# Dynamic convolution, Fourier mixing and MLP on one core: 64-bit weights turned into float32 by four VectorE operations and two ScalarE operations instead of seven VectorE operations

## The chip, the cores and the metric

The kernel runs on one core of a Trainium2 chip. The metric is the device time of one launch in microseconds (us), the median of several runs. TensorE multiplies matrices into PSUM; VectorE (DVE), ScalarE (ACT) and GpSimd (POOL) work elementwise; SyncE (SP) issues the DMAs.

## The reference, cut to what matters

```python
# x (8, 4224, 192) f32, weight_gen (8, 4224, 8, 7) f32, w_ch1 (192, 768) f64, w_ch2 (768, 192) f64
w = softmax(weight_gen, axis=-1)
out = np.einsum('bshk,bskhg->bshg', w, x_unf)        # 7 taps, 8 heads of 24 channels
X = np.fft.fft(np.fft.fft(x, axis=1), axis=2)        # x is that output
u = x + np.real(X).astype(np.float32)
un = (u - mean(u)) / np.sqrt(var(u) + 1e-06)
ch = np.maximum(un @ w_ch1, 0.0) @ w_ch2
return (u + ch).astype(np.float32)
```

The two weight matrices come as 64-bit floats: a float32 array times a 64-bit scalar. The kernel reads them as pairs of 32-bit words and makes float32 of them on the chip.

## The kernel before, in words

For each of 8 batches the kernel does a convolution (softmax of the taps, products on VectorE, sums on GpSimd, for batch 0 also products on ScalarE and sums on TensorE), folds rows and takes a first transform on TensorE (`spectrum`), writes the spectrum to DRAM and reads it back turned (`transform`, tiles g2, results pp), copies pp to pq on ScalarE (L945 to L956), and then for 9 groups of 512 rows mixes (`mix`, PSUM tile eo), normalises (`norm`) and runs the two matmuls of the MLP (`mlp`: L1105 into ph, relu on ScalarE into tiles hh, L1149 into po). There are 72 groups. The MLP needs the weights as pairs of float16 (w1h, w1l, w2h, w2l), and w2 first as float32 (w2f) for the first six groups.

The weights are loaded once, in six raw pieces of 128 x 384 numbers of two words each (`load_piece`), three of w1 and three of w2. `words_to_f32` (L485) turns a piece into float32 by seven VectorE operations: L492 and L494 make sign, exponent and upper mantissa from the high word, L495 and L496 set numbers too small for float32 to zero, L498 takes the power of two of the result, L501 scales the low word by it, L503 adds. `split_f32` (L506) then makes the float16 pair of a w1 piece, one ScalarE operation (L508) and one VectorE operation (L509). `prep_w1` does the three w1 pieces after the last convolution product of batch 0, `prep_w2` one w2 piece each, in the stretch before the first MLP group.

The program is written in one order, and `plan` (L175) then sets the order of every engine's queue: a list scheduler with the costs of `cost`, which ranks the operations over several walks, keeps the best walk, and links each queue in that order. `held` (L391) makes instructions wait in this order behind a given one, but only those on the same engine as that one (L204). Tiles of one tag are given out in the order in which the program first uses them: tag hh has 10 buffers (temporaries of the conversion, then the relu results), ph has 3 PSUM banks, po has 2. `keep_warm` puts 40 small matmuls (L563) on TensorE while the spectrum of batch 0 goes to DRAM and back, and 8 more after each of two mix steps.

Of the kernel before, what the change touches and what calls it, by code (L numbers as in the profile page):

```python
# [11 lines left out]
F16 = mybir.dt.float16  # L12
F32 = mybir.dt.float32
I32 = mybir.dt.int32
U32 = mybir.dt.uint32
AF = mybir.ActivationFunctionType
ALU = mybir.AluOpType
# [4 lines left out]
P = 128  # L22
# [21 lines left out]
DVE_ADDS = {(1, c): 1 for c in range(2, NC)}  # L44
HOLD3 = 3
WIRE = 0.7

F32_GROUPS = 6
WIDE_FROM = 2
# [89 lines left out]
def together(ap):  # L139

    run = 1
    for step, n in reversed(ap.ap[1:]):
        if n > 1 and step != run:
            break
        run *= n
    return run


def cost(ins, lane, reads, writes):
# [10 lines left out]
    if lane == "sp":  # L160
        if ins.opcode == "DmaTransposeAnt":
            return TURN * n / (12 * P), 2000 + 1.2 * n, 1.09 * n
        size, run = BYTES[out.dtype], min(together(ap) for ap in reads + writes)
        return 400, 2000 + WIRE * count(out) * size, out.ap[0][1] * count(out) / run * (0.5 + 0.0023 * run * size)
    if lane == "dve":
# [196 lines left out]
def tile_dynconv_fnet_mlp(  # L362
# [12 lines left out]
    nc = tc.nc  # L375
# [22 lines left out]
    def pst(tag, bufs, shape, dt, name):  # L398
        return ps.tile(shape, dt, tag=tag, name=name, bufs=bufs)
# [44 lines left out]
    PW = 2 * D  # L444
# [7 lines left out]
    def temp(nm, dt):  # L452
        return sb.tile([P, PW], dt, tag="hh", name=nm, bufs=10)
# [31 lines left out]
    def words_to_f32(raw, out, nm, bank):  # L485

        hi, lo = raw[:, :, 1], raw[:, :, 0]
        v = nc.vector
        a = pst(*bank, [P, PW], I32, f"pa_{nm}")
        w = pst(*bank, [P, PW], F32, f"pw_{nm}")  # L490
        t = temp(f"t_{nm}", I32)
        v.tensor_scalar(out=a, in0=hi, scalar1=3, scalar2=0x3FFFFFFF,  # L492
                        op0=ALU.logical_shift_left, op1=ALU.bitwise_and)
        v.scalar_tensor_tensor(out=t, in0=hi, scalar=-0x40000000, in1=a, op0=ALU.bitwise_and, op1=ALU.bitwise_or)  # L494
        v.tensor_scalar(out=a, in0=hi, scalar1=0x7FF00000, scalar2=None, op0=ALU.bitwise_and)  # L495
        v.scalar_tensor_tensor(out=w, in0=a, scalar=float(0x38100000), in1=t.bitcast(F32),  # L496
                               op0=ALU.is_ge, op1=ALU.mult)
        v.tensor_scalar(out=a, in0=w.bitcast(I32), scalar1=23, scalar2=23,  # L498
                        op0=ALU.logical_shift_right, op1=ALU.logical_shift_left)
        r = t.bitcast(F32)  # L500
        ins = v.scalar_tensor_tensor(out=r, in0=lo.bitcast(U32), scalar=2.0 ** -52, in1=a.bitcast(F32), op0=ALU.mult, op1=ALU.mult)  # L501
        out = w if out is None else out
        last_word.append(v.tensor_tensor(out=out, in0=w, in1=r, op=ALU.add))  # L503
        return out

    def split_f32(w, hi16, lo16, sc):  # L506

# [18 lines left out]
    def prep_w1(raws):  # L526
        s1 = weight_scale([raw[:, :, 1] for raw in raws], 64, "w1")
        scales.append(s1)
        hi, lo = temp("w1h_1", F16), temp("w1l_1", F16)
        w = words_to_f32(raws[0], None, "w1_1", ("ph", 3))  # L530
        split_f32(w, hi, lo, s1)
        with held(g2_loads[0, (NK1 + 2) // 3 // TRI * TRI].ins):
            for src, dst in ((hi, w1h1), (lo, w1l1)):
                for i in range(2):
                    for j in range(2):
                        nc.sync.dma_start(dst[64 * j:64 * j + 64, i * PW:(i + 1) * PW], src[64 * i:64 * i + 64])
        for i in range(2):
            cs_ = slice(i * PW, (i + 1) * PW)
            w = words_to_f32(raws[1 + i], None, f"w1_0{i}", ("ph", 3))
            split_f32(w, w1h0[:, cs_], w1l0[:, cs_], s1)  # L540

    def prep_w2(i):
        words_to_f32(loaded[1][i], w2_part(i)[0], f"w2_{i}", ("ph", 3) if i < 2 else ("po", 2))
# [653 lines left out]
    last_word, last_split, last_lo, last_bn, last_ph, scales = [], [], {}, {}, {}, []  # L1197
# [119 lines left out]
```

## Time and profile before

| what | value |
|---|---|
| time, median of 3 runs (lowest to highest) | 1079.35 us (1078.82 to 1079.69) |
| profiled execution: span from first to last instruction | 1076.2 us |
| median of the runs less that span | 3.15 us |
| TensorE busy | 1057.1 us (98%) |
| VectorE busy | 933.7 us (87%) |
| ScalarE busy | 862.9 us (80%) |
| GpSimd busy | 851.4 us (79%) |
| granted TensorE clock, mean | 0.998 |

The span is the time between the program's first and last instruction in the one execution that was profiled; the runs' times hold what lies around it too. The profile's page gives busy time by engine, the span in 40 slices, the chain of work that ended last and the costliest groups of instructions; the trace behind it can be asked for stretches, lines and tiles.

### The profile page before, as it was taken

The page shows a single profiled execution, that of the slowest core. Times are in us where ns is not written, and L with a number is a line of the kernel's source. Part 1 is how long each engine was busy: PE and PEld are TensorE (multiplying, and loading weights), DVE is VectorE, ACT ScalarE, POOL GpSimd, SP SyncE. Part 2 cuts the span into 40 slices and gives each one's busy share as a digit, 9 for nine tenths or more (in the row PEclk, how much of TensorE's full clock was granted, in tenths as well). Part 3 has the DMA queues.
Part 4 walks back from the last instruction along what each step waited for, and adds up shares of the span by engine and source line. Part 5 has one row for each costly group of instructions (what it writes and reads, how often), then busy time and mean ns, then how long its engine had stood idle before and what let it go on. Part 6 is the DMA issues. An engine that isn't in the chain of part 4 may idle for free.

```text
span 1076.2 us, 23645 instructions
## 1 busy us (share of the span) xinstructions
PE 1057.1 (98%) x8603; PEld 803.8 (75%) x8603; DVE 933.7 (87%) x1597; ACT 862.9 (80%) x2597; POOL 851.4 (79%) x616
## 2 busy tenths in 40 slices
PE   8899999999999999999999999999999999999998
PEld 5476687886778777887778777787778777886667
DVE  8999999999989998899989998899989997374433
ACT  4666875669987998889897898889897998699953
POOL 5979899899969999699959999699969999011210
PEclk9999999999999999999999999999999999999999
DMA  9453056624683458625582447734583424523221
GB/s 322 136 147 117 8 136 180 175 48 101 157 233 80 98 133 210 158 75 121 145 215 80 111 127 205 157 76 125 137 180 89 88 68 99 143 56 87 72 71 49
DMA packets 186324, 134.88 MB, mean 125 GB/s; under 512 B 134299, under 2 KB 167008, under 8 KB 186208
## 3 DMA queue, kind: packets, MB, share of 16 engines
q1 hardware_dynamic: 186208, 133.37, 48.3%
q8 instruction: 68, 1.11, 0.4%
q14 instruction: 48, 0.39, 0.1%
HBM read 61.46 MB, written 39.37 MB: 94 GB/s over the span
## 4 chain that ended last, share of the span: by engine, by line
PE 66%; POOL 15%; DVE 10%; issue 5%; ACT 2%; DMA 1%; SPq 0%; POOLq 0%; DVEq 0%; ACTq 0%
PE po L1149 28%; PE ph L1105 24%; POOL u L893 7%; POOL u L822 4%; PE pp L941 4%; PE eo L972 3%; PE ph L1072 3%; PE pg L845 3%; DVE pr L810 2%; POOL sm L836 2%; POOL hl L1048 1%; DVE pr L889 1%; DVE u L889 1%; DMA x_sb<-in_x_dram 1%; POOL hl L1050 1%
## 5 line engine op out<-in xcount | busy, mean ns | idle before, releaser
L893 POOL TENSOR_TENSOR u<-u,pr 128x1536 f32<-128x1536 f32 x144 | 497.1, 3454 | 15.4 <-DVE pr L889 13.4
L1149 PE MATMUL po<-w2h,hh 128*128 128x192 f16 x2880 | 411.2, 246 | 1.3 <-ACT po L1146 0.8
L1149 PEld LDWEIGHTS <-hh 128*128 128x128 f16 x4320 | 364.1, 98 | 61.6 <-issue 18.9
L1105 PE MATMUL ph<-ht,w1h 128*128 128x512 f16 (+1 forms) x1296 | 387.5, 362 | 2.6 <-DVE hh L1125 1.2
L1149 PE MATMUL po<-w2l,hh 128*128 128x192 f16 x1440 | 354.1, 246 | 0.0
L1125 DVE SCALAR_TENSOR_TENSOR hh<-ph,hh 128x512 f16<-128x512 f32 (+1 forms) x396 | 241.3, 634 | 77.5 <-ACT hh L1124 76.9
L889 DVE TENSOR_TENSOR pr<-x_sb,wp 128x1536 f32<-128x1536 f32 x144 | 250.2, 1743 | 6.8 <-POOL u L893 6.7
L1124 ACT ACTIVATE hh<-ph 128x512 f16<-128x512 f32 (+1 forms) x396 | 208.8, 551 | 48.5 <-PE ph L1105 27.1
L1105 PEld LDWEIGHTS <-w1h 128*128 128x128 f16 x1296 | 126.9, 100 | 94.8 <-issue 16.9
L1105 PE MATMUL ph<-ht,w1l 128*128 128x512 f16 (+1 forms) x528 | 180.4, 350 | 0.0
L1038 ACT ACTIVATE un<-u,rs 128x192 f32<-128x192 f32 x252 | 122.0, 539 | 16.4 <-POOL rs L1036 13.1
L1048 POOL TENSOR_TENSOR hl<-un,hl 128x512 f16<-128x512 f32 (+1 forms) x69 | 74.3, 1077 | 74.8 <-ACT hl L1042 39.5
L822 POOL TENSOR_TENSOR u<-u,pr 128x768 f32<-128x768 f32 (+1 forms) x72 | 115.6, 1612 | 8.8 <-DVE rs L1012 4.7
L1009 ACT ACTIVATE junk<-u,st 128x192 f16<-128x192 f32 x252 | 114.2, 453 | 3.0
L1007 ACT ACTIVATE junk<-u 128x192 f16<-128x192 f32 x252 | 90.8, 360 | 21.9 <-DVE u L981 17.5
L972 PEld LDWEIGHTS eo<-cs_sb,pq 97*128 97x128 f32 x544 | 93.4, 191 | 9.0 <-issue 1.1
L972 PE MATMUL eo<-cs_sb,pq 97*128 97x97 f32 x544 | 92.3, 265 | 0.1
L810 DVE TENSOR_TENSOR pr<-x_sb,wp 128x768 f32<-128x768 f32 (+1 forms) x91 | 74.6, 867 | 1.4 <-PE pa L815 0.7
L1105 PEld LDWEIGHTS <-w1l 128*128 128x128 f16 x528 | 52.9, 100 | 23.7 <-issue 3.7
L1036 POOL TENSOR_TENSOR rs<-st,rs 128x4 f32<-128x4 f32 (+1 forms) x69 | 14.0, 202 | 67.8 <-DVE rs L1012 63.1
L836 POOL TENSOR_TENSOR sm<-u 128x382 f32<-128x382 f32 x64 | 64.0, 1000 | 3.4 <-ACT u L689 3.2
L845 PE MATMUL pg<-sm,f_sb 128*128 128x192 f32 x256 | 55.1, 333 | 1.4 <-POOL sm L837 1.3
(143 smaller groups left out, 1585.5 us busy)
## 6 DMA issues: line engine op xcount, KB each, us to landing
out_dram<-u SPq DMA_DIRECT2D x64, 384.0 KB
x_sb<-in_x_dram SPq DMA_DIRECT2D x48, 384.0 KB
g<-g_d SPq DMA_DIRECT2D x40, 336.0 KB
x_sb<-in_x_dram SPq DMA_DIRECT2D x8, 864.0 KB
g_d<-gt SPq DMA_DIRECT2D x32, 195.0 KB
g_d<-gt SPq DMA_DIRECT2D x32, 189.0 KB
w<-in_weight_gen_dram SPq DMA_DIRECT2D x6, 924.0 KB
x_sb<-in_x_dram SPq DMA_DIRECT2D x8, 672.0 KB
```

The lines of the kernel that those rows point to most:

```text
L810: last_product[b] = nc.vector.tensor_tensor(out=dst, in0=rows, in1=wk, op=ALU.mult)
L822: adder.tensor_tensor(out=u, in0=u, in1=pr, op=ALU.add)
L889: last_product[b] = nc.vector.tensor_tensor(out=pr.rearrange("p (s r) (h g) -> p s (r h) g", s=2, g=G), in0=rows, in1=wp[:, :, :, k:k + 1] ...
L893: nc.gpsimd.tensor_tensor(out=u, in0=u, in1=pr, op=ALU.add)
L972: last_mix[b] = nc.tensor.matmul(eo[:, e, j, :], lhsT=pq[0:DH, e, r, r:r + P], rhs=cs_sb[:, e, :], start=True, stop=True)
L1007: nc.scalar.activation(junk, uv[t], AF.Identity, scale=-1.0 / D, accum_out=st[:, t, 0:1])
L1009: nc.scalar.activation(junk, uv[t], AF.Square, bias=st[:, t, 0:1], accum_out=st[:, t, 1:2])
L1038: nc.scalar.activation(un[:, t, :], uv[t], AF.Identity, bias=rs[:, 1, t:t + 1], scale=rs[:, 0, t:t + 1])
L1105: last_ph[n] = nc.tensor.matmul(ph[:, 0:T], lhsT=wt[:, cs_], rhs=ht[:, 0:T, blk], start=(i == 0 and not opens), stop=(i == len(terms) - 1 ...
L1124: nc.scalar.activation(a[:, 0:T], ph[:, 0:T], AF.Relu)
L1125: nc.vector.scalar_tensor_tensor(out=l[:, 0:T], in0=ph[:, 0:T], scalar=0.0, in1=a[:, 0:T], op0=ALU.max, op1=ALU.subtract)
L1149: nc.tensor.matmul(po[t // 2][:, t % 2, :], lhsT=hx[:, t], rhs=wx[:, c2, :], start=(c2 == 0 and i == 0 and not seeds[t // 2] and not (late ...
```

## The change

A piece is now made so: ScalarE takes the absolute value of the high word read as float32, scaled by a constant that rounds to zero in float16 below the least number kept (near), and the sign of that (keep, 0 or 1, float16). VectorE shifts the high word (as L492 does), then joins the low word's upper three bits, then sign and top exponent bit, and last multiplies by keep. The intermediate stays in one PSUM tile; the PSUM tile of the result is made only where the result isn't written to w2f directly, and the temporary t of tag hh goes, for near and keep of the same tag. The low word's other bits are dropped where the old form rounded them in.

```diff
+LEAST = float(np.float32(2.0 ** -25) / np.nextafter(np.uint32(0x38100000).view(np.float32), np.float32(0)))
 
         hi, lo = raw[:, :, 1], raw[:, :, 0]
         v = nc.vector
+        near, keep = temp(f"near_{nm}", F16), temp(f"keep_{nm}", F16)
+        nc.scalar.activation(near, hi.bitcast(F32), AF.Abs, scale=LEAST)
+        nc.scalar.activation(keep, near, AF.Sign)
         a = pst(*bank, [P, PW], I32, f"pa_{nm}")
-        w = pst(*bank, [P, PW], F32, f"pw_{nm}")
-        t = temp(f"t_{nm}", I32)
+        w = pst(*bank, [P, PW], F32, f"pw_{nm}") if out is None else out
         v.tensor_scalar(out=a, in0=hi, scalar1=3, scalar2=0x3FFFFFFF,
                         op0=ALU.logical_shift_left, op1=ALU.bitwise_and)
-        v.scalar_tensor_tensor(out=t, in0=hi, scalar=-0x40000000, in1=a, op0=ALU.bitwise_and, op1=ALU.bitwise_or)
-        v.tensor_scalar(out=a, in0=hi, scalar1=0x7FF00000, scalar2=None, op0=ALU.bitwise_and)
-        v.scalar_tensor_tensor(out=w, in0=a, scalar=float(0x38100000), in1=t.bitcast(F32),
-                               op0=ALU.is_ge, op1=ALU.mult)
-        v.tensor_scalar(out=a, in0=w.bitcast(I32), scalar1=23, scalar2=23,
-                        op0=ALU.logical_shift_right, op1=ALU.logical_shift_left)
-        r = t.bitcast(F32)
-        ins = v.scalar_tensor_tensor(out=r, in0=lo.bitcast(U32), scalar=2.0 ** -52, in1=a.bitcast(F32), op0=ALU.mult, op1=ALU.mult)
-        out = w if out is None else out
-        last_word.append(v.tensor_tensor(out=out, in0=w, in1=r, op=ALU.add))
-        return out
+        v.scalar_tensor_tensor(out=a, in0=lo, scalar=29, in1=a, op0=ALU.logical_shift_right, op1=ALU.bitwise_or)
+        v.scalar_tensor_tensor(out=a, in0=hi, scalar=-0x40000000, in1=a, op0=ALU.bitwise_and, op1=ALU.bitwise_or)
+        last_word.append(v.tensor_tensor(out=w, in0=a.bitcast(F32), in1=keep, op=ALU.mult))
+        return w
```

## Rows read from the trace of the kernel before

**Rows 1.** The page's first part: busy us, share of the span, instructions.

```profile
PE 1057.1 (98%) x8603; PEld 803.8 (75%) x8603; DVE 933.7 (87%) x1597; ACT 862.9 (80%) x2597; POOL 851.4 (79%) x616
```

**Rows 2.** Busy us by stretch: length, PE, PEld, DVE, ACT, POOL; then clock, DMA.

```profile
71.40:91.80 20.40, 19.55 (x181) 18.34 (x180) 19.99 (x46) 9.60 (x34) 18.90 (x12) 1.00 0.51 135
91.80:111.60 19.80, 18.09 (x112) 11.67 (x111) 19.40 (x66) 13.78 (x31) 19.80 (x13) 1.00 0.31 100
111.60:330.00 218.40, 214.21 (x1571) 165.08 (x1570) 209.64 (x353) 167.77 (x490) 199.97 (x150) 1.00 0.53 136
330.00:1050.00 720.00, 719.05 (x6298) 551.08 (x6297) 611.44 (x1010) 618.00 (x1840) 558.86 (x390) 1.00 0.48 117
```

**Rows 3.** PE's waits, 95 to 330 us: us in total, times, longest.

```profile
PE po L1149 <- DVE u L1158: 1.2, 1, 1.2
...
PE tr L1028 <- DVE t_w L501: 0.3, 1, 0.3
...
PE ph L1105 <- ACT hh L1120: 0.3, 1, 0.3
```

**Rows 4.** Chain that ended last, 55 to 130 us: start, us, what.

```profile
71.47 0.48 DVE pa_w L492
...
91.28 0.56 DVE w2f L503
91.84 0.29 DVE eo L978
```

**Rows 5.** Timeline of DVE: start us, length us, line, operation, tiles, shapes.

```profile
79.91 0.55 DVE L501 SCALAR_TENSOR_TENSOR t_w<-raw_w,pa_w 128x384 f32<-128x384 uint32 x1
80.37 0.55 DVE L495 TENSOR_SCALAR pa_w<-raw_w 128x384 int32<-128x384 int32 x1
80.96 0.57 DVE L496 SCALAR_TENSOR_TENSOR pw_w<-pa_w,t_w 128x384 f32<-128x384 int32 x1
...
108.26 1.50 DVE L598 TENSOR_REDUCE wp<-w 128x184 f32<-128x1288 f32 x1
```

**Rows 6.** DVE's groups by form, 71 to 112 us: count, busy us, mean ns.

```profile
L492 DVE TENSOR_SCALAR pa_w<-raw_w 128x384 int32<-128x384 int32 x6 | 3.3, 554 | 0.1
...
L501 DVE SCALAR_TENSOR_TENSOR t_w<-raw_w,pa_w 128x384 f32<-128x384 uint32 x6 | 3.3, 549 | 0.1
...
L503 DVE TENSOR_TENSOR w2f<-pw_w,t_w 128x384 f32<-128x384 f32 x3 | 1.6, 550 | 0.0
```

**Rows 7.** ACT's groups by form, 60 to 112 us.

```profile
L508 ACT ACTIVATE w1h<-pw_w,sc_w 128x384 f16<-128x384 f32 x3 | 1.8, 597 | 3.5 <-DVE pw_w L503 3.4
...
L689 ACT COPY u<-pa 128x384 f32<-128x384 f32 x3 | 1.4, 474 | 0.0
```

**Rows 8.** Timeline of ACT; in brackets the idle time before and what ended it.

```profile
70.83 1.28 ACT L1210 ACT_TABLE_LOAD   x1
...
75.71 0.58 ACT L508 ACTIVATE w1h<-pw_w,sc_w 128x384 f16<-128x384 f32 x1 [3.38 <-DVE pw_w L503]
80.62 0.33 ACT L945 COPY pq<-pp 97x204 f32<-97x204 f32 x1 [4.32 <-PE pp L941]
...
83.22 0.58 ACT L508 ACTIVATE w1h<-pw_w,sc_w 128x384 f16<-128x384 f32 x1
...
90.98 0.32 ACT L977 COPY ot<-eo 128x194 f32<-128x194 f32 x1 [0.78 <-PE eo L972]
...
104.55 0.60 ACT L1120 ACTIVATE hh<-ph 128x512 f32<-128x512 f32 x1
```

**Rows 9.** Timeline of PE.

```profile
79.69 0.85 PE L941 MATMUL pp<-te_sb,g 102*97 102x99 f32 x8
...
84.42 0.93 PE L941 MATMUL pp<-to_sb,g 102*97 102x99 f32 x8 [0.35 <-ACT pq L956]
...
99.23 0.38 PE L1105 MATMUL ph<-ht,w1h 128*128 128x512 f16 x1 [0.56 <-ACT ht L1029]
```

## The prediction, made before the changed kernel ran

> **What bounds the kernel now.** I read the page's busy times first, then four stretches, then the waits of TensorE, then the chain that ended last around the conversions, and last the queues of VectorE, ScalarE and TensorE there. The busy times alone would mislead: TensorE stands at 98% and VectorE at 87% [rows 1], but an average hides that the conversions all lie before the MLP runs at full rate. In the stretches [rows 2] the reader is to see two regimes. From 330 to 1050 us TensorE is busy 719.05 of 720 us, so 0.95 us of idle time is all that anything could win there. From 71.4 to 111.6 us VectorE is the full engine (19.99 of 20.40 us, then 19.40 of 19.80), while TensorE's busy time in the first of the two is partly keep-warm filler. Between them, from 111.6 to 330 us, TensorE is idle for 218.40 - 214.21 = 4.19 us. So after the first MLP matmul at 99.23 us [rows 9] the kernel ends when TensorE has done its fixed work; a change in the start is worth what it moves that matmul forward, plus what it takes out of TensorE's few waits. Those are short: the longest of 95 to 330 us is 1.2 us, and a conversion operation (L501) is named in one of 0.3 us [rows 3]. The chain of waits runs through VectorE's conversions from 71.47 us up to the mix at 91.84 us [rows 4]. That looks like 20 us bound by conversions, but it is nearly a tie: the second transform's results come at the same time. ScalarE's copy of eo, which the mix also needs, starts at 90.98 and lasts 0.32 us [rows 8], so the mix could start at 91.30 us at best.
>
> **The change part by part.**
>
> VectorE, before the mix. Five of the six pieces are converted from 71.4 to 91.8 us, 35 operations in the old form and 20 in the new, so 15 go. An operation lasts 0.549 to 0.554 us by its group [rows 6], but they overlap: an independent one starts 0.46 us after the one before it (80.37 - 79.91), a dependent one 0.59 us after (80.96 - 80.37) [rows 5]. So 6.9 to 8.9 us of VectorE's time goes. The kept operations cost what they cost now: the join of the low word has the kinds of operands of L494, and the multiply by keep those of L503 at 0.550 us [rows 6], except for a float16 operand, which the trace does not show in such a multiply; I bound it by 0.474 and 0.597 us, the ScalarE rows of like size [rows 7], and take 0.55 because the operation is nearest to L503. Six of them make at most 0.5 us either way, which the freed time covers. What is late next is the transform: the mix can move from 91.84 to 91.30 us, 0.54 us, and the other 6 or 8 us become idle time of VectorE in front of it. Little else can fill it: the convolution of batch 1 on VectorE is held behind the first groups' normalisation, and the sixth piece's PSUM tile comes, in the order of the tag po, after those of the second group's transposes. GpSimd is 18.90 of 20.40 us busy there already [rows 2].
>
> ScalarE. Twelve operations of 128 x 384 come. The trace has none that reads every second word; the nearest are a plain copy at 0.474 us and the scaled one with a per-partition factor at 0.597 us [rows 7]. I take 0.5 us, nearer the copy since scale is a constant here: 6.0 us in all (5.7 to 7.2). They need only the raw words, which lie in SBUF long before, and they are not held, since a hold binds only instructions of the engine that it names. The cover is ScalarE's idle time of 3.38 us before L508 at 75.71 and 4.32 us before L945 at 80.62 [rows 8], 7.70 us together, so I cost them at nothing. Without that cover they would stand before the copies to pq, for which the transform waits. The order of tag hh lets the second pair start only after the first piece's float16 pair has its tiles, about 75 us, so some could slip past 80.6. In the other direction, the L508 at 83.22 us now stands among those copies, and TensorE waits 0.35 us for one of them at 84.42 [rows 8, 9]; with the w1 pieces done sooner it moves into the idle time. I take 0.3 us of gain from that (0 to 0.35).
>
> The wait that comes. The fourth VectorE operation waits for keep on ScalarE. Behind it stand the next piece's operations and L509, and behind L509 the w1 rows' DMAs; these are queued on SP behind the spectrum's loads, so their start does not move. With VectorE 7 us ahead of need, a wait here costs nothing until it exceeds that.
>
> The sixth piece, after 104 us. Three operations go, 3 x 0.46 = 1.4 us on a full VectorE. It holds one PSUM tile of po instead of two, so the transposes that wait 0.3 us for L501 [rows 3] go on. In the tag hh its temporary stood before the relu results, and the first relu starts only at 104.55 us [rows 8], just when the sixth piece is begun; near and keep can be placed far earlier, so TensorE's 0.3 us wait for a relu [rows 3] should go as well. TensorE idles 19.80 - 18.09 = 1.71 us in this stretch [rows 2]; I take 0.6 us of it (0 to 1.7).
>
> The convolution of batch 1. Its first VectorE operation, at 108.26 us [rows 5], can start 0.54 + 0.3 + 1.4 = 2.2 us sooner. It matters only through TensorE's waits from 111.6 to 330 us. As the order of all queues is planned anew, these waits fall out anew: I take zero, bounded by a gain of 2.2 us (what comes sooner cannot save more) and a loss of 4.2 us (the idle time once more).
>
> The sum: 0.54 + 0.3 + 0.6 + 0 = 1.4 us less. The profiled execution's span of 1076.2 us becomes 1074.8; the median of the runs lies 3.15 us above that span and goes with it, to 1077.9 us. The 9 us taken from VectorE thus shrink to 1.4, because most of it is taken where VectorE was ahead of nothing but a tie.
>
> A rule of the skill on ScalarE's tables. Between the table load at 70.83 us (1.28 us, for the square root) and the end of these rows, copies and a relu ran without another [rows 8]. The Trainium skill, "ScalarE: Activation LUTs", section "Table sets: the hidden batching unit", says that cheap functions stand in every table set and that a function outside the active set needs a load; it names relu, copy, identity and abs, and does not name sign there. The trace agrees for relu and copy; no row shows abs or sign. By the rule the two cost no load if sign is among the cheap ones, and the sum stays 1.4 us; if it is not, the case is the fourth rival.
>
> **The rivals.**
>
> First, the larger gain: VectorE's 2.2 us reach TensorE. For it: VectorE is 209.64 of 218.40 us busy from 111.6 to 330 us [rows 2], and the waits there name VectorE first [rows 3]. Against it: GpSimd is 199.97 us busy in the same stretch, and the waits are few. At full effect 0.54 + 0.35 + 1.7 + 2.2 = 4.8 us go, 1074.6 us; in the middle, 3.3 us, 1076.0.
>
> Second, nothing moves: the transform starts at 79.69 us [rows 9] in any case, as the spectrum's way through DRAM is untouched, and the new order of ScalarE eats the fractions: 1079.3 us. For it: every term of my sum is under a microsecond.
>
> Third, the other side: slower. Convolution products that are ready sooner on VectorE are put ahead of the evictions that TensorE waits for. The place is the stretch from 111.6 to 330 us, the price the row where TensorE waits 1.2 us for L1158 [rows 3]. Three such waits more (3.6 us) outweigh my 1.4 us by the 2.2 us that can be told; with four it is 4.8 - 1.4 = 3.4 us slower, 1082.7. For it: the queues are planned by estimated durations. Against: from 330 us on the same planner leaves TensorE 0.95 us of idle time.
>
> Fourth, the change doesn't do what it says on ScalarE: sign needs a load and the way back, 2 x 1.28 us [rows 8], each time it is used apart. With three such stretches, 7.7 + 6.0 us meet 20.40 - 9.60 = 10.80 us of idle ScalarE time [rows 2]: 2.9 us late at the mix, less the 0.6 us after it, 1081.7 us. The same 2.9 us come from six operations more than I count standing before the copies to pq.
>
> **How the numbers follow.** A difference of 0.2%, 2.2 us, is about what a measurement of this kernel can tell from none: faster is below 1077.2 us, slower above 1081.5. My forecast (0.3 to 2.1 us less) has 0.38, nothing moves 0.12, both within that bound: same 0.50. The larger gain has 0.34: faster 0.34. The third rival has 0.11 and the fourth 0.05: slower 0.16. The range is 1075.0 to 1081.0 us: it leaves out the far end of the larger gain and most of the two slower cases. The likeliest case's own range is 1077.2 to 1079.0 us.
>
> **What would show it.** VectorE's conversions end near 85 us and it idles before the mix, which starts near 91 us; ScalarE's twelve operations lie before 81 us at about 0.5 us each, with no table load more; the first MLP matmul stands near 98.4 us and the first relu before 104 us; L598 of the large part near 106 us; TensorE's idle time from there to 330 us is about 4 us. The forecast is wrong if the first MLP matmul does not move, if that idle time changes by more than 2 us, or if abs or sign brings loads.

## The result and the profile after

The changed kernel takes 1088.17 us (median of 4 runs, 1087.41 to 1089.36) against 1079.09 us (4 runs, 1078.26 to 1079.69) for the kernel before on the same chip: ratio 1.0086 [1.0072, 1.01], 9.1 us slower. The forecast was 1077.9 us with a range up to 1081.0. The profiled execution is the slowest of the four (1089.36 us); its span is 1087.6 us, 11.4 us above the 1076.2 us of before. That is 2.3 us more than the medians differ by, so the traces overstate the loss a little.

The page's first part, as [rows 1]:

```profile
PE 1059.7 (97%) x8603; PEld 806.7 (74%) x8603; DVE 928.4 (85%) x1579; ACT 866.2 (80%) x2609; POOL 851.8 (78%) x616
```

The stretches of [rows 2], and three of 5 us in which the largest single loss lies (length, then busy us of PE, PEld, VectorE, ScalarE and GpSimd, then the granted clock):

```profile
71.40:91.80 20.40, 19.92 (x183) 18.66 (x182) 13.42 (x34) 15.00 (x44) 19.64 (x13) 1.00 0.55 145
91.80:111.60 19.80, 16.81 (x112) 11.41 (x110) 18.89 (x62) 13.50 (x31) 19.80 (x13) 1.00 0.31 102
111.60:330.00 218.40, 211.24 (x1517) 161.50 (x1516) 205.68 (x344) 163.87 (x473) 189.23 (x142) 0.99 0.50 127
330.00:1050.00 720.00, 715.10 (x6264) 550.29 (x6262) 614.36 (x1011) 616.15 (x1852) 569.13 (x397) 1.00 0.50 119
...
185.00:190.00 5.00, 0.92 (x6) 0.69 (x5) 5.00 (x2) 0.84 (x2) 5.00 (x5) 1.00 0.54 206
190.00:195.00 5.00, 4.39 (x13) 1.70 (x13) 4.93 (x10) 0.95 (x2) 3.84 (x9) 0.66 0.38 113
195.00:200.00 5.00, 5.00 (x29) 3.56 (x27) 2.91 (x5) 4.49 (x7) 0.00 (x0) 1.00 0.27 103
```

VectorE lost work as intended: 19.99 us of the first stretch became 13.42. But TensorE's idle time (length less its busy time) grew in every later stretch: from 1.71 to 2.99 us, from 4.19 to 7.16, from 0.95 to 4.90. From 185 to 190 us TensorE is busy for only 0.92 us while VectorE shows two operations in 5 us.

Three of TensorE's waits over the whole run (us in total, times, longest):

```profile
...
PE ph L1102 <- DVE w2l L549: 4.7, 1, 4.7
PE ph L1102 <- DMA ht<-hl: 2.5, 2, 1.4
PE tr L1025 <- DVE ht L1028: 1.9, 1, 1.9
```

In [rows 3] the longest wait was 1.2 us. VectorE's queue, with the lines that answer to [rows 5]:

```profile
84.04 1.01 DVE L500 TENSOR_TENSOR w2f<-pa_w,keep_w 128x384 f32<-128x384 f32 x2
...
92.21 0.37 DVE L975 TENSOR_TENSOR eo<-eo,ot 128x194 f32<-128x194 f32 x1 [7.16 <-ACT ot L974]
...
183.57 0.15 DVE L1009 RECIPROCAL rs<-rs 128x1 f32<-128x1 f32 x1
183.64 6.38 DVE L551 TENSOR_TENSOR fsc<-sc_w,sc_w 128x1 f32<-128x1 f32 x1
189.94 0.15 DVE L551 TENSOR_TENSOR isc<-sc_w,sc_w 128x1 f32<-128x1 f32 x1
190.01 1.01 DVE L549 TENSOR_TENSOR w2l<-ws,w2h 128x384 f16<-128x384 f32 x2
```

The first five conversions end at 85.05 us and VectorE then idles 7.16 us until the mix, as foretold. The surprise is at 183.64 us: a product of 128 x 1 numbers lasts 6.38 us, where a reciprocal of the same size just before it lasts 0.15. It is not one of the changed operations. L551 (L554 of before) multiplies the two scales of w1 and w2; both operands lie in SBUF. In its queue it stands ahead of the float16 pieces w2l, and the MLP's matmuls wait for the PSUM banks of tag ph that these free. The planner could not see this: `cost` prices an operation of VectorE by its number of elements, 150 + 1.042 ns for this one, and has no term for where its operands lie or for what GpSimd does. TensorE's queue, as [rows 9]:

```profile
81.08 0.90 PE L938 MATMUL pp<-te_sb,g 102*97 102x99 f32 x8
...
99.69 0.38 PE L1102 MATMUL ph<-ht,w1h 128*128 128x512 f16 x1 [0.56 <-ACT ht L1026]
...
103.08 0.63 PE L1025 MATMUL tr<-ident,un 128*128 128x128 f32 x4 [1.93 <-DVE ht L1028]
...
190.61 0.48 PE L1102 MATMUL ph<-ht,w1h 128*128 128x512 f16 x1 [4.69 <-DVE w2l L549]
...
192.16 0.63 PE L1102 MATMUL ph<-ht,w1l 128*128 128x512 f16 x1
192.59 0.63 PE L1102 MATMUL ph<-ht,w1h 128*128 128x512 f16 x1
```

After the 4.69 us of idle time the matmuls start 0.43 us apart (192.16, 192.59), twice the distance at full clock (99.69 and 99.91 us in the same queue), and the granted clock of that window is 0.66. In half-microsecond windows it is 1.00 up to 190.5 us, 0.50 in each from 191.0 to 194.0, and 1.00 again from 194.5: 0.50 is the lower level, 1.2 GHz. By (1 - 0.66) x 5 I estimate 1.7 us more for it.

ScalarE's new operations by form (count, busy us, mean ns), as [rows 7], with the first relu from its timeline:

```profile
L492 ACT ACTIVATE near_w<-raw_w 128x384 f16<-128x384 f32 x6 | 3.3, 552 | 0.0
L493 ACT ACTIVATE keep_w<-near_w 128x384 f16<-128x384 f16 x6 | 3.1, 522 | 0.1
```

```profile
106.64 1.54 ACT L1117 ACTIVATE hh<-ph 128x512 f32<-128x512 f32 x3
```

GpSimd while VectorE's product is held:

```profile
183.14 4.15 POOL L819 TENSOR_TENSOR u<-u,pr 128x768 f32<-128x768 f32 x3
187.24 1.01 POOL L833 TENSOR_TENSOR sm<-u 128x382 f32<-128x382 f32 x1
188.19 1.81 POOL L819 TENSOR_TENSOR u<-u,pr 128x768 f32<-128x768 f32 x1
189.94 0.21 POOL L834 TENSOR_TENSOR sm<-u 128x2 f32<-128x2 f32 x1
```

The product ends at 190.02 us, when the sum that starts at 188.19 has ended at 190.00. It did not slip in where earlier operations ended: the first row holds three, which end at 184.98, 185.53 and 187.29, and the second ends at 188.25. (The profile's spans on GpSimd are rough.)

Of the 11.4 us of the span, the first MLP matmul is 0.46 us later (99.69 against 99.23). From there to the end TensorE is idle for 17.59 us instead of 9.23, 8.36 more, and busy for 970.32 us instead of 967.74, 2.58 more, with the same 8165 matmuls; 1.7 of that is the lower clock, and 0.9 I did not assign.

Two theories stood at this point. One: the plan of the queues, made anew, put a product with two SBUF operands beside a run of GpSimd ('lock' in the expectations below), and lost more elsewhere ('order'); the new operations are innocent. The rival, 'work': the operations themselves (their waits across ScalarE and VectorE, their tiles) cost the time.

### The profile page after: what moved, and what is told of

The parts are those of the page before. It is cut to its first block, busy times and chain, and to the rows that moved or that the text cites. A ratio compares the mean times of both kernels' runs of the same rounds, so it can differ in the third digit from the quotient of the medians.

```text
span 1087.6 us, 23643 instructions
## 1 busy us (share of the span) xinstructions
PE 1059.7 (97%) x8603; PEld 806.7 (74%) x8603; DVE 928.4 (85%) x1579; ACT 866.2 (80%) x2609; POOL 851.8 (78%) x616
## 4 chain that ended last, share of the span: by engine, by line
PE 61%; POOL 12%; DVE 10%; issue 6%; ACT 4%; DMA 2%; SPq 0%; DVEq 0%; POOLq 0%; ACTq 0%
PE po L1146 25%; PE ph L1102 22%; POOL u L890 9%; PE pp L938 4%; PE eo L969 3%; PE ph L1069 3%; DVE pr L886 3%; PE pg L842 3%; DMA ht<-hl 2%; DVE hh L1122 2%; PE warm L560 1%; POOL hl L1045 1%; POOL sm L833 1%; DVE u L886 1%; PE pa L812 1%
```

## The experiments

**The product in another form, order of after.** Only L551 changes; on every engine the trace has the operations in the order of after.

```diff
-            nc.vector.tensor_tensor(out=both, in0=scales[0][:, i:i + 1], in1=s2[:, i:i + 1], op=ALU.mult)
+            nc.vector.tensor_scalar(out=both, in0=scales[0][:, i:i + 1], scalar1=s2[:, i:i + 1], scalar2=None, op0=ALU.mult)
```

> The changed kernel with every queue in the same order; only the two 128x1 products fsc and isc (L551) are written as tensor_scalar with a per-partition factor in place of tensor_tensor. Theory 'lock': the product fsc took 6.38 us at 183.64 us since it reads both operands from SBUF while GpSimd runs back to back; TensorE waited 4.69 us for w2l behind it and ran at a granted clock of 0.66 afterwards. Then both products take about 0.15 us, the wait and the lower clock go, and the time falls by 4.7 + some 2 us to about 1081. Theory 'order' (the new order of the queues alone) and theory 'work' (the new operations alone) both expect 1088, unchanged, since neither order nor conversions differ.

Measured: 1081.92 us (1081.44 to 1082.46), ratio to before 1.003 [1.0018, 1.0041]. That is 6.25 us less than after (6.0 by the two ratios to before). VectorE's queue and two stretches:

```profile
183.29 0.20 DVE L551 TENSOR_SCALAR fsc<-sc_w,sc_w 128x1 f32<-128x1 f32 x1
183.54 0.56 DVE L549 TENSOR_TENSOR w2l<-ws,w2h 128x384 f16<-128x384 f32 x1
```

```profile
190.00:195.00 5.00, 5.00 (x29) 3.56 (x27) 3.78 (x11) 4.77 (x8) 3.49 (x8) 1.00 0.23 83
...
330.00:1050.00 720.00, 716.28 (x6273) 550.78 (x6270) 610.05 (x1008) 614.54 (x1840) 561.74 (x394) 1.00 0.49 118
```

The hold, the wait for w2l and the low clock go together, and 4.69 + 1.7 = 6.4 us is about what goes. The idle time after 330 us does not: 3.72 us, so it is another matter.

**The same edit in the kernel before.** Does the edit win anything by itself?

```diff
-            nc.vector.tensor_tensor(out=both, in0=scales[0][:, i:i + 1], in1=s2[:, i:i + 1], op=ALU.mult)
+            nc.vector.tensor_scalar(out=both, in0=scales[0][:, i:i + 1], scalar1=s2[:, i:i + 1], scalar2=None, op0=ALU.mult)
```

> The kernel before with the same two products as tensor_scalar, every queue in the same order. Theory 'lock': they took 1.39 and 0.62 us there, 0.3 us in the new form; TensorE waited little behind them, so 0.3 to 1.0 us less: about 1078.5, within what can be told from none. 'Order' and 'work': 1079.

Measured: 1078.49 us (1077.81 to 1078.93), ratio 0.9994 [0.9986, 1.0003]: nothing that can be told. In the kernel before, the two products were held as well, but for less, and none of TensorE's waits names w2l. Its queue of VectorE, and GpSimd's operations at the time:

```profile
182.27 1.39 DVE L554 TENSOR_TENSOR isc<-sc_w,sc_w 128x1 f32<-128x1 f32 x1
183.58 0.62 DVE L554 TENSOR_TENSOR fsc<-sc_w,sc_w 128x1 f32<-128x1 f32 x1
```

```profile
181.83 1.80 POOL L822 TENSOR_TENSOR u<-u,pr 128x768 f32<-128x768 f32 x1
183.60 0.58 POOL L822 TENSOR_TENSOR u<-u,pr 128x192 f32<-128x192 f32 x1
```

Here each product ends with one operation of GpSimd: at 183.66 us, when the sum of 181.83 has ended at 183.63, and at 184.20, when the next has ended at 184.18.

**The product as before, but one operand in PSUM, order of after.** Which is it, the form of the instruction or where its operands lie?

```diff
-        every = pst("ph", 3, [P, 3], F32, f"me_{nm}")
+        every = pst("ph", 3, [P, 5], F32, f"me_{nm}")
...
+            nc.vector.tensor_copy(out=every[:, 3:5].bitcast(I32), in_=sc)
+            return sc.bitcast(F32), every[:, 3:5]
...
-            nc.vector.tensor_tensor(out=both, in0=scales[0][:, i:i + 1], in1=s2[:, i:i + 1], op=ALU.mult)
+            nc.vector.tensor_tensor(out=both, in0=scales[0][:, i:i + 1], in1=s2p[:, i:i + 1], op=ALU.mult)
```

> The changed kernel with every queue in its own order; the products fsc and isc (L551) stay tensor_tensor, but their second operand comes from PSUM, where one added copy of two columns puts it just before. Theory 'two SBUF operands' (a tensor_tensor that reads both operands from SBUF waits for GpSimd's run): the products take about 0.15 us and the time is that of after_scalar, 1082 us (1081.4 to 1082.5, plus up to 0.2 for the copy). Rival 'the form' (a 128x1 tensor_tensor waits there, wherever its operands lie): fsc takes 6.4 us again and the time stays at 1088.

Measured: 1082.48 us (1082.32 to 1082.95), ratio 1.0035 [1.0023, 1.0048]. VectorE's queue:

```profile
183.24 0.14 DVE L636 TENSOR_TENSOR fsc<-sc_w,me_w 128x1 f32<-128x1 f32 x1
```

The same instruction at the same place, beside the same GpSimd work, lasts 0.14 us once its second operand comes from PSUM. So the product was held for reading both operands from SBUF. The Trainium skill says so in "SBUF — State Buffer", section "Who interferes with whom": a VectorE instruction with two SBUF inputs contends with a GpSimd instruction that reads SBUF, and one with at most one such input, outside the modes that use two ports, does not. The runs agree on which instruction is held (6.38 against 0.14 us). The same page, section "Summary: rules for kernel authors", has the second one to issue blocked until the first finishes. The kernel before agrees with that (1.39 and 0.62 us, each to the end of one GpSimd operation); in after the hold went past the ends of four, so a hold can be longer than that sentence allows.

**The new operations in the old order.** Every queue has the order of the kernel before, read from a table. The four VectorE operations of a piece stand where the first four of the seven stood; near and keep of the first piece stand on ScalarE before the square root's first use, the others after the first L508.

```diff
-    order = best[2]
+    order = {}
+    for lane, text in QUEUES.items():
+        steps = np.frombuffer(zlib.decompress(base64.b85decode(text)), "<i2")
+        line = sorted(queued[lane], key=lambda ins: program[ins.name])
+        order[lane] = [line[k] for k in np.cumsum(steps)]
```

> The changed kernel's operations with every queue in the order of the kernel before: each common operation at its old place, the four VectorE operations of a piece at the places of the first four of the old seven, near and keep on ScalarE ahead of L1210's root (first piece) and behind the first L508 (the other five). Theory 'order': the loss goes and the small gain of the first sum is left, 1077 to 1079.5 us. Theory 'work': 1088 stays. Theory 'lock': it depends on how long the product fsc or isc is held this time; with 1 to 2 us as before, 1078; with 6 us, 1084.

Measured: 1077.46 us (1076.78 to 1078.71), ratio 0.9988 [0.9979, 0.9996], 1.3 us faster than before. Its queues of VectorE and of TensorE, and its stretches (line numbers are some 80 higher):

```profile
91.18 0.37 DVE L1058 TENSOR_TENSOR eo<-eo,ot 128x194 f32<-128x194 f32 x1 [3.06 <-ACT ot L1057]
```

```profile
98.67 0.38 PE L1185 MATMUL ph<-ht,w1h 128*128 128x512 f16 x1 [0.57 <-ACT ht L1109]
```

```profile
91.80:111.60 19.80, 18.57 (x115) 11.80 (x114) 19.33 (x64) 14.51 (x32) 19.80 (x13) 1.00 0.30 101
111.60:330.00 218.40, 213.94 (x1580) 165.78 (x1579) 208.26 (x350) 167.92 (x491) 201.01 (x151) 1.00 0.54 136
330.00:1050.00 720.00, 719.05 (x6293) 550.37 (x6292) 610.58 (x1009) 617.85 (x1839) 557.94 (x389) 1.00 0.48 117
```

This is about the sum of the prediction, 1.4 us less, which took the new plan at nothing; the interval of the 1.3 us is 0.4 to 2.3. The first MLP matmul comes 0.56 us sooner (98.67 against 99.23) and TensorE's idle time to 111.6 us falls from 1.71 to 1.23 us. From there to the end the stretches hold 4.46 and 0.95 us of idle time, as before (4.19 and 0.95). So in this order the rival theory falls: four with two cost no more than seven.

**The old operations in the order of after.** The reverse: seven operations together at the place of the last of the four.

```diff
-    order = best[2]
+    order = {}
+    for lane, text in QUEUES.items():
...
```

> The old seven operations with every queue in the order of the changed kernel (the seven stand together at the place of the last of the four; near and keep are left out). Theory 'order': slow as the changed kernel, 1086 to 1089 us. Theory 'work': 1079. Theory 'lock': if the product is held as in the changed kernel, 1088; if it is held shorter, about 1081 to 1082.

Measured: 1107.58 us (1103.15 to 1108.5), ratio 1.0269 [1.0255, 1.0283], far from what was expected. From its timeline of VectorE and from TensorE's waits:

```profile
197.40 6.38 DVE L636 TENSOR_TENSOR fsc<-sc_w,sc_w 128x1 f32<-128x1 f32 x1
```

```profile
PE pp L1023 <- ACT pq L1038: 7.6, 1, 7.6
...
PE ph L1187 <- DVE w2l L634: 4.8, 1, 4.8
```

In the order of after the three operations of L508 all stand on ScalarE ahead of the copies to pq, and here each waits for seven operations where after has four: the copies begin at 88.02 us instead of 82.07, and TensorE waits 7.6 us for them. The rest of the extra time I did not take apart. So the total says what seven operations cost in an order made for four with two, and not what the change is worth. What the run does show is the hold: without any new operation, this order gives the product the same 6.38 us and TensorE a wait of 4.8 us. GpSimd ran the same sequence beside it, and the product ended 0.02 us after the same one of its sums (203.78 against 203.76 us).

**Both: the old order and the product as tensor_scalar.** New operations as in the fourth experiment, L551 as in the first.

```diff
-            nc.vector.tensor_tensor(out=both, in0=scales[0][:, i:i + 1], in1=s2[:, i:i + 1], op=ALU.mult)
+            nc.vector.tensor_scalar(out=both, in0=scales[0][:, i:i + 1], scalar1=s2[:, i:i + 1], scalar2=None, op0=ALU.mult)
```

> The changed kernel's operations in the order of the kernel before, and the two products fsc and isc as tensor_scalar. In after_in_before they took 1.05 and 0.63 us, now 0.4 us together; TensorE waited under 0.5 us behind them, so 1077.0 us, 0 to 0.5 less than after_in_before; the best of these kernels if the theories 'order' and 'lock' both hold. 'Work' expects nothing of it.

Measured: 1077.56 us (1076.64 to 1078.74), ratio 0.9982 [0.997, 0.9993]. It can't be told from the run without the scalar form. These two have the lowest medians measured, and the intervals of both exclude the time of the kernel before.

**Other plans for both forms.** How much does a plan made anew vary by itself? The planner has a number, PATIENCE, for how long it may leave VectorE idle for an operation of higher rank: 120 ns in both kernels. It was set to 140 and to 100, in both kernels, each with the product as tensor_scalar, so that a hold of it plays no part.

```diff
-PATIENCE = {"dve": 120}
+PATIENCE = {"dve": 140}
```

> before_scalar with one constant of the planner changed (PATIENCE of VectorE 140 in place of 120), so all queues are planned anew while no operation changes. Theory 'lottery' (any new plan of this planner lands some us away, whatever the operations): moves by more than 2 us from 1078.5, most likely up, 1079 to 1086. Theory 'systematic' (the new operations make worse plans, the old ones don't): stays at 1078 to 1080.

> The same with PATIENCE 100. 'Lottery': moves by more than 2 us from 1078.5, most likely up. 'Systematic': 1078 to 1080.

> after_scalar with PATIENCE 140: the new operations, planned anew once more, the products as tensor_scalar. 'Lottery': anywhere from 1076 to 1086, as likely below 1081.9 as above. 'Systematic': 1081 to 1084.

> after_scalar with PATIENCE 100: a third plan of the new operations beside 1081.9 (120) and 1078.1 (140). 'Lottery': lands somewhere between 1077 and 1088, as the old operations did with 1078.5, 1085.8 and 1085.7. 'Systematic' (the new operations plan worse than the old): above the old operations' 1085.7 at the same constant.

Measured, with the runs at 120 from above:

| PATIENCE | seven operations | four and two |
|---|---|---|
| 100 | 1085.71 us, 1.0061 [1.0048, 1.0075] | 1081.07 us, 1.0019 [1.001, 1.0029] |
| 120 | 1078.49 us, 0.9994 [0.9986, 1.0003] | 1081.92 us, 1.003 [1.0018, 1.0041] |
| 140 | 1085.79 us, 1.0061 [1.0046, 1.0077] | 1078.13 us, 0.9991 [0.9982, 1.0] |

The two slow plans of the seven operations lose in different places: at 140 TensorE is idle for 5.84 us from 330 to 1050 us, in many small waits, where it was 1.20 at 120; at 100 it waits 4.94 us at one place, and the clock is down for a while after that. The stretch at 140, then TensorE's timeline at 100:

```profile
330.00:1050.00 720.00, 714.16 (x6248) 549.21 (x6245) 609.89 (x1007) 614.84 (x1838) 562.04 (x391) 1.00 0.48 118
```

```profile
182.38 0.47 PE L469 MATMUL me_w<-m_w,ones 1*128 1x1 f32 x2 [4.94 <-DVE wp L729]
```

With the same operations, 20 ns of planning patience moves the time by 7.3 us (1085.79 - 1078.49). By these times, with the planner's number at 120 the seven had a good plan and the four a middling one; at 100 and at 140 the four are the faster by 4.6 and 7.7 us. Three plans each are too few for a mean, but they exclude that the new operations are the slower ones in every plan.

## Why the prediction was wrong

**The step that failed** is the term for the stretch from 111.6 to 330 us: "As the order of all queues is planned anew, these waits fall out anew: I take zero, bounded by a gain of 2.2 us ... and a loss of 4.2 us". The place was right; zero was wrong, and so was the upper bound. The idle time there rose by 3.0 us, inside the bound, but the 4.69 us wait in it cost 1.7 us of clock as well, which a bound on idle time doesn't count: 4.7 us together. What the runs showed in place of the zero is one tiny product held beside GpSimd; as tensor_scalar it gives 6.25 us back.

**The same step was left out after 330 us.** The 0.95 us of idle time [rows 2] was read as all that could be won there; that the new plan might lose there was not costed. It lost 3.95 us, of which TensorE's two waits for ht from a DMA are 2.5. With the product as tensor_scalar 3.72 us of idle time stay. In the old order it is 0.95 again.

**The start of the transform.** The second rival took it as fixed ("the transform starts at 79.69 us [rows 9] in any case"), and so did my sum. In after it starts at 81.08: the new plan orders even the convolution of batch 0 anew, ahead of every changed operation (the first near starts at 69.28 us). VectorE's last product of it and its last operation of the spectrum, before and then after:

```profile
62.54 0.95 DVE L810 TENSOR_TENSOR pr<-x_sb,wp 128x768 f32<-128x768 f32 x1 [0.34 <-PE pa L815]
...
71.12 0.34 DVE L855 TENSOR_TENSOR gt<-pg,up 128x190 f32<-128x190 f32 x1
```

```profile
63.74 0.95 DVE L807 TENSOR_TENSOR pr<-x_sb,wp 128x768 f32<-128x768 f32 x1 [0.71 <-PE pa L812]
...
72.45 0.35 DVE L852 TENSOR_TENSOR gt<-pg,up 128x190 f32<-128x190 f32 x1
```

Both come later by 1.2 to 1.3 us, and the transform, which reads that spectrum back from DRAM, starts 1.39 us later than in [rows 9]. With the same operations in the old order it starts at 79.75. From the transform's start to the mix, after takes 92.21 - 81.08 = 11.13 us, before 91.75 - 79.69 = 12.06: 0.93 us less, where 0.54 + 0.3 = 0.84 was forecast. So that gain came, and the later start took back more.

**The terms that held.** VectorE's four operations last 0.55 us each, twelve on ScalarE 0.552 and 0.522 us (6.4 us in all, within 5.7 to 7.2); the first five conversions end at 85.05 us. The table loads number 16 in both profiles (8, 7 and 1 by line), so the fourth rival falls. The Trainium skill, "ScalarE: Activation LUTs", section "Table sets: the hidden batching unit", names abs among the cheap functions that stand in every set; the trace agrees, and shows that sign needed no load here either. In the old order the mix moves from 91.75 us to 91.18, 0.57 us for 0.54 forecast; the line of before is

```profile
91.75 0.36 DVE L978 TENSOR_TENSOR eo<-eo,ot 128x194 f32<-128x194 f32 x1
```

The whole comes to 1.3 us for 1.4, but not term by term. The 0.3 us for L508 did not come there, as that order keeps one among the pq copies, at 83.03 us. And the 1.71 us from which 0.6 us was taken hold 0.91 us ahead of the first MLP matmul, whose move the sum had already counted; behind it TensorE's idle time falls from 0.80 to 0.49 us, 0.3 for 0.6. The 0.56 us at that matmul and this 0.3 make 0.9 us in the trace, whose span is 1.0 us shorter (1075.2); that the medians give 1.3 is within their interval, and part of the agreement with 1.4 is luck.

**The terms that did not.** In after, where 0.6 us of gain was taken for 91.8 to 111.6 us, 1.3 us more idle time came; the 1.93 us wait of the transposes for ht at 103.08, which the plan of before has not, is alone more than that. The first relu came at 106.64 us, where before 104 was foretold.

**The rivals.** The first, the larger gain, had 0.34; nothing of it came, not even in the old order, where the stretch from 111.6 to 330 us keeps 4.46 us of idle time. The third, slower, had the right side, stretch and kind (VectorE's order makes TensorE wait) at 0.11. Its mechanism was wrong: no eviction stood behind convolution products four times. One tiny product stood behind GpSimd's sums, four times as dear as the 1.2 us that I priced a wait at [rows 3].

**The sum by cause.** The held product and the clock behind it: 6.25 us (1088.17 to 1081.92, shown by changing that product alone; with the operand in PSUM and one copy more it is 5.7). The rest of the plan: 1081.92 - 1077.46 = 4.5 us (shown by the old order, which takes it away). The operations: -1.3 us (1077.46 against 1078.8 in the same comparison). These add up to 9.4 us because each step starts where the last one ends, so the 9.1 us measured side by side is no test of the split. The -1.3 us also holds for the old order alone: in the order of after, seven operations took 1107.58 us and four with two 1088.17.

What stays open: why the hold lasted past several ends of GpSimd operations in after and ended with the first in before; whether the operations save as much in a typical plan as in the old order; which of the edit's effects (durations, tiles, number of operations) turned the planner to this plan, since none of them was tried by itself; and why one of the 21 runs of the kernel before in the later comparison took 1085.59 us, 6.5 above their median, for which there is no trace.

## What to carry to other kernels

Where a planner writes the order of the queues, a small edit is two changes: the operations, and a new plan. Measure the edit with the old order frozen, and price the new plan from the scatter of plans (here 7 us) rather than at zero. And before trusting an order, look in the trace for VectorE operations of a few elements that last over 1 us: two SBUF operands beside a busy GpSimd had here a wait of up to 6.38 us, differing with the order, which an operand in PSUM or a per-partition scalar took away. A planner whose costs lack that wait cannot avoid it.

## What the runs showed of the hardware that was not expected

- A product of 128 x 1 numbers with both operands in SBUF lasted 6.38 us beside GpSimd's sums, the same 6.38 us in two kernels at different times (183.64 and 197.40) beside the same sequence of them; 1.39 and 0.62 us in the kernel before, each to the end of one GpSimd operation; 0.14 us with one operand in PSUM; 0.20 us as tensor_scalar with a scalar in SBUF.
- TensorE idle for 4.69 us was followed by a window of 5 us with a granted clock of 0.66 and by 1.00 in the next 5 us: by my estimate 1.7 us on top of the wait. After the wait of 4.94 us with seven operations at 100 the clock was 0.61 and 0.53 in the two windows of 2 us from 182 to 186 us: by the same estimate 1.7 us again.
